# Dense-matmul tiles on 128-byte starts, second MoE in chunks of 384 and 512 tokens, nine x pairs, new planner keys

## The chip, the core and the metric

The kernel runs on one core of a Trainium2 chip. The metric is the device time of one execution in microseconds; lower is better. TensorE (PE) multiplies, VectorE (DVE), ScalarE (ACT) and GpSimd (POOL) do the elementwise work, and SyncE (SP) issues nearly all transfers.

## The reference, cut to what matters

Attention over 4 batches of 8 heads, with a band of 32 positions to each side and 32 global tokens, gives `x` with 4 x 544 = 2176 tokens of 512 features. Two dense blocks follow:

```python
h = np.maximum(x @ w_in, 0.0)                   # 512 -> 1024
conv = sum(conv_w[k] * shifted(h, k - 1) for k in range(3))
x = h * sigmoid(conv) @ w_out                   # 1024 -> 512
xk, xr = (mu * x + (1 - mu) * x_prev for mu in (mu_k, mu_r))
k = np.maximum(xk @ w_k, 0.0)                   # 512 -> 1024
out = sigmoid(xr @ w_r) * (k * k @ w_v)         # 512 -> 512, 1024 -> 512
```

## The kernel before, in words

**Dense matmuls.** Every operand of a dense product is split into a rounded high part and a low rest (`hi`, `lo`, type float32r, 4 bytes an element), and each product is the sum of three matmuls: hi x hi, hi x lo, lo x hi. One matmul holds a 128x128 block as the stationary operand and streams a moving operand of up to 512 columns past it. The five kinds are named by their PSUM tile:

- `ph` (line 955): w_in stationary, the x tiles moving, 482 columns (262 in the last chunk); 480 matmuls
- `po` (line 1044): w_out stationary, the gate tiles `gh`/`gl` moving, 480 columns (260 in the last chunk); 480
- `pk` (line 1187): w_k stationary, `xkh`/`xkl` moving, as many columns as the chunk has tokens; 96 a chunk, 576 in all
- `pr` (line 1251): `xrbuf` stationary, w_r moving, 512 columns; 12 for each of 17 blocks of 128 tokens, 204 in all
- `pv` (line 1288): `k2h`/`k2l` stationary, w_v moving, 512 columns; 24 a block, and 48 of 256 columns for the last block, 432 in all

That is 2172 matmuls with 941,760 columns.

**First MoE.** `dense(b)` works through five chunks of tokens (`CW`, 480 and last 260 wide): `ph` for eight groups of 128 hidden features, then ReLU, a convolution of three taps, sigmoid, product and split on DVE, ACT and POOL, then `po` for four groups, stored to DRAM. The attention of batch b+1 runs in between. An attention unit is two heads: scores `s`, softmax, transposes `pe`, products `o`, normalization `xn`, a transpose `X` (line 633), and copies of `X` into the x pairs of up to two chunks. `XB` = 10 x pairs (ring `x0` for hi, `x1` for lo) are held by four feature blocks of a chunk each until the chunk's last `ph`.

**Second MoE.** `moe2()` cuts the 2176 tokens into chunks of 384, 384, 384, 384, 384 and 256. Each loads its x, forms a difference `d`, the mixes `xk` and `xr` and their splits, then runs all its `pk`, `pr` and `pv` in that order. Behind each of the eight `pk` groups of a chunk stand a ReLU into `robuf` (line 1203), a square (1208), and the split into `k2h` (1215) and `k2l` (1220). The x tiles of this part use the rings `x0` and `x1` too.

**Order of the work.** A planner (`Plan`) simulates the five engines from a cost for each task and emits every engine's order at build time. Among tasks that could start within `WINDOW` it takes the one with the smallest key. Keys are due times: `s_key` for attention (`T_START`, `STEP0`, `T_DENSE`, `SLOT`, `LEAD`, `GAP`, `GAP1`), `d_key` for the dense part, and what these imply for all that they need, transfers included. Elementwise tasks may have two or three engines to go to; the one that finishes first after adding a bias (`DVE_BIAS`, `ACT_BIAS`, `POOL_BIAS`) gets it, with another bias in each phase of time (`PHASES`). `mmr(n)` = n / 2.4 + 13.3 ns is the planner's cost of a dense matmul; a `pr` group of six costs 40 ns more. The order is static: an engine waits at the head of its list.

**Where tiles lie.** Tiles are laid one behind another in SBUF with each size rounded up to 32 bytes. In a partition, the constants end at byte 3360, which is 32 past a multiple of 128, and what follows inherits it. The starts of the dense matmuls' operands, as remainders after division by 128:

| operand | remainder |
|---|---|
| w_in, w_out, later w_v, xrbuf (blocks 512 or 2048 bytes apart) | 32 |
| w_k, w_r | 96 |
| x pairs, 1952 bytes apart: the ring of hi; of lo | 32, 64, 96, 0, 32, ...; 96, 0, 32, 64, ... |
| `gh`/`k2h` (first half; second half, 1928 bytes on) | 32; 40 |
| `gl`/`k2l` (the four buffers; their second halves) | 32, 64, 96, 0; 40, 72, 104, 8 |

For chunk 0 the x tiles of feature blocks k = 0 to 3 start at 32, 64, 32, 0 (hi) and 96, 0, 96, 64 (lo).

Of the kernel before, what the change touches and what calls it, by code (L numbers as in the profile page):

```python
# [10 lines left out]
F32 = mybir.dt.float32  # L11
F32R = mybir.dt.float32r
I32 = mybir.dt.int32
# [6 lines left out]
DM = H * D  # L20
FF = 1024
P = 128
# [5 lines left out]
CW = (480, 480, 480, 480, 260)  # L28
NC = len(CW)
CA = tuple(sum(CW[:c]) for c in range(NC + 1))  # L30
XW = max(CW) + 2
CH0 = 512
XO = max(CW[0] + 1, max(CW[1:]))
TOK = B * S
CH = 384
SCALE = 0.125
BIG = 8.0e9
HUGE = 3.0e38
# [1 line left out]
EST = 256  # L40
# [9 lines left out]
W2_BUFS = 3  # L50
W2R_BUFS = 3
E_STEP = 16
XB = 10
T_START = -32416
STEP0 = 7098
T_DENSE = 24497
SLOT = 58775
LEAD = -7520
GAP = 16998
GAP1 = -7474  # L60
STEPS_H = 6
E_BUFS = 4
H_FRAC = 0.5
LAG_TE = -5130
LAG_PV = 87927
LAG_G = -19574
LEAD_Q = 2184
S_COST = 960
M_COST = 845
E_COST = 1182  # L70
PV_COST = 470
LAG_TX = 11192
WINDOW = 114
FILL_MIN = 309
FILL_MARGIN = 3249
FILL_START = 6
FILL_RATE = 0.624
PENALTY = 4050
AHEAD = 1405
PHASES = (-313483, 41538, 302764, 460459)  # L80
DVE_BIAS = (425, 13181, -112, 8785, 3254)
ACT_BIAS = (-8199, -1203, -224, -20768, -16631)
POOL_BIAS = (24870, -34502, -354, -10831, 5828)
H_BUFS = 5
C_BUFS = 3
G_BUFS = 4
# [330 lines left out]
def mmr(n):  # L417
    return max(119.0, n / 2.4 + 13.3)
# [3 lines left out]
def attn_moe_kernel(  # L422
# [51 lines left out]

    ident = const.tile([P, P], F32, name="ident")
    fold = const.tile([P, 64], F32, name="fold")
    zero = const.tile([P, 1], F32, name="zero")
    mask = const.tile([P, 4, P], F32, name="mask")
    convw = const.tile([P, 3 * FT], F32, name="convw")
    mus = const.tile([P, 2 * KT], F32, name="mus")  # L480
# [174 lines left out]
    def x_alloc(u):  # L655
        b, k = divmod(u, NP)
        for c, *_ in windows(b, 0, S):
            if ("x", c, k) in bufs:
                continue
            bufs["x", c, k] = [buf("x0"), buf("x1")]  # L660
            blank = [z - CA[c] + 1 for z in [GAPPED] + [(S + 1) * i - 1 for i in range(B + 1)] if CA[c] - 1 <= z <= CA[c + 1]]

            def fn(c=c, k=k, blank=blank):
                for i, x in enumerate(bufs["x", c, k]):
                    t = alloc(x, [P, XW], F32R, f"x{i}_{c}_{k}")
                    for z in blank:
                        nc.gpsimd.tensor_copy(t[:, z : z + 1], zero)

            ev["xa", c, k] = add("POOL", 130 * len(blank), fn, take=bufs["x", c, k], name=f"xa{c}_{k}")
            ev["x", c, k] = []  # L670
# [148 lines left out]
    def narrow_tasks(nm, src, n, braw, bmag, after):  # L819
        state = {}  # L820

        def fload():
            state["raw"] = alloc(braw, [P, max(n, EST), 2], I32, f"{nm}r")
            halves = state["raw"].bitcast(I16).rearrange("p n t -> p (n t)")
            part, words = skewed(src), 4 * n - 1
            step = 4 * EST
            for c in range(0, words, step):
                end = min(c + step, words)
                load_to(out=halves[:, c:end], in_=part[:, c:end])

        def fzero():
            state["mag"] = alloc(bmag, [P, max(n, EST)], F32, f"{nm}m")[:, :n]
            nc.gpsimd.memset(state["mag"], 0.0)

        def fhead():
            head = state["mag"].bitcast(F16).rearrange("p (n t) -> p n t", t=2)[:, :, 1]
            top = state["raw"].bitcast(BF16).rearrange("p n (t u) -> p n t u", u=2)[:, :n, 1, 0]
            nc.scalar.copy(head, top)

        def ftail():  # L840
            bits = state["mag"].bitcast(I32)
            nc.vector.scalar_tensor_tensor(
                bits, state["raw"][:, :n, 0], 13, bits, op0=ALU.logical_shift_right, op1=ALU.bitwise_or
            )

        f = n / WST
        a = add("DMA", 1250 * f, fload, deps=after, take=[braw], name=f"ld{nm}")
        z = add("POOL", 150 + 326 * f, fzero, deps=[a], take=[bmag], name=f"zero{nm}")
        c = add("ACT", 60 + 581 * f, fhead, deps=[a, z], use=[bmag, braw], name=f"abs{nm}")
        c = add("DVE", 68 + 534 * f, ftail, deps=[c], use=[bmag, braw], name=f"low{nm}")  # L850
        return c, state
# [221 lines left out]


    outf = out.rearrange("b s d -> (b s) d")
    widths = (384, 384, 384, 384, 384, 256)
    chunks = [(sum(widths[:i]), n) for i, n in enumerate(widths)]
    big = {}

# [14 lines left out]
    def moe2():  # L1094
# [5 lines left out]
        def chunk(ci, tok, n):  # L1100
# [12 lines left out]
            for m in range(KT):  # L1113
                bx, bd = buf("h"), buf("c")

                def fld(bx=bx, m=m):
                    t = alloc(bx, [P, XW + 2], F32, f"x2_{ci}_{m}")
                    for c, lo, hi in spans:
                        lead = int(c == 0)
                        load_to(out=t[:, lo - first : hi - first], in_=x2d[c][m][:, lead + lo - CA[c] : lead + hi - CA[c]])  # L1120

                def fd(e, bx=bx, bd=bd, m=m):
                    d = alloc(bd, [P, XW], F32, f"d{ci}_{m}")
                    e.tensor_sub(d[:, 0 : wd - 1], bx.tile[:, 1:wd], bx.tile[:, 0 : wd - 1])

                src = [ev["x2", c, m] for c, *_ in spans]
                ld = add("DMA", 900, fld, deps=src + [ev["relu", NC - 1]], take=[bx], name=f"ldx{ci}_{m}")
                d = add("DVE", tt(n), lambda fd=fd: fd(nc.vector), deps=[ld], take=[bd], use=[bx], name=f"d{ci}_{m}",
                        alts=[("POOL", 100 + 2.27 * n, lambda fd=fd: fd(nc.gpsimd))])
                for i, nm in ((0, "xk"), (1, "xr")):  # L1130
                    bt = buf("x0")

                    def fx(bt=bt, bx=bx, bd=bd, i=i, nm=nm, m=m):
                        x = alloc(bt, [P, XW], F32, f"xt{ci}{nm}{m}")
                        for o0, i0, sn in segs:
                            nc.vector.scalar_tensor_tensor(
                                x[:, o0 : o0 + sn], bd.tile[:, i0 : i0 + sn], mus[:, KT * i + m : KT * i + m + 1],
                                bx.tile[:, i0 : i0 + sn], op0=ALU.mult, op1=ALU.add,
                            )

                    x = add("DVE", tt(n) + 70, fx, deps=[d], take=[bt], use=[bx, bd], name=f"x{nm}{ci}_{m}")
                    if nm == "xk":
                        bh, bl = buf("x0"), buf("x1")

                        def fh(copy, bh=bh, bt=bt, m=m):
                            copy(alloc(bh, [P, XW], F32R, f"xkh{ci}_{m}")[:, :n], bt.tile[:, :n])

                        def fl(e, bh=bh, bl=bl, bt=bt, m=m):
                            lo = alloc(bl, [P, XW], F32R, f"xkl{ci}_{m}")
                            e.tensor_sub(lo[:, :n], bt.tile[:, :n], bh.tile[:, :n].bitcast(F32))  # L1150

                        h = add("ACT", 40 + act(n), lambda fh=fh: fh(nc.scalar.copy), deps=[x], take=[bh], use=[bt],
                                name=f"xkh{ci}_{m}",
                                alts=[("DVE", 67 + 0.52 * n, lambda fh=fh: fh(nc.vector.tensor_copy))])
                        l = add("DVE", tt(n), lambda fl=fl: fl(nc.vector), deps=[h], take=[bl], use=[bt, bh],
                                name=f"xkl{ci}_{m}", alts=[("POOL", 100 + 2.27 * n, lambda fl=fl: fl(nc.gpsimd))])
                        xk.append([h, l])
                        xkb.append((bh, bl))
                    else:
                        def fh(copy, bt=bt, m=m):  # L1160
                            copy(big["rx"][:, m, :n], bt.tile[:, :n])

                        def fl(e, bt=bt, m=m):
                            e.tensor_sub(
                                big["rx"][:, KT + m, :n], bt.tile[:, :n], big["rx"][:, m, :n].bitcast(F32)
                            )

                        h = add("ACT", 40 + act(n), lambda fh=fh: fh(nc.scalar.copy), deps=[x, free_out] + prev_xr,
                                use=[bt], name=f"xrh{ci}_{m}",
                                alts=[("DVE", 67 + 0.52 * n, lambda fh=fh: fh(nc.vector.tensor_copy))])  # L1170
                        l = add("DVE", tt(n), lambda fl=fl: fl(nc.vector), deps=[h], use=[bt],
                                name=f"xrl{ci}_{m}", alts=[("POOL", 100 + 2.27 * n, lambda fl=fl: fl(nc.gpsimd))])
                        xr.append([h, l])
# [67 lines left out]
            for j in range(nt):  # L1241
# [11 lines left out]
                                start=(k == 0 and i == 0), stop=(k == KT - 1 and i == 2),  # L1253
                            )

                cost = 6 * mmr(DM) + 40
                last = mm_group(
                    f"R{ci}_{j}", bp, 2, part,
                    [[z for k in (2 * q, 2 * q + 1) for z in xr[k] + wrr_done[k, 0]] for q in range(2)],
# [179 lines left out]
```

## Time and profile before

| | |
|---|---|
| runs | 547.84, 551.41, 551.53 us; median 551.41 |
| the profiled execution | 550.57 us, of which its span is 548.8 |
| TensorE busy | 525.0 us, 96% of the span |
| VectorE, ScalarE, GpSimd busy | 321.5, 295.0, 177.4 us |
| mean granted TensorE clock | 0.988 of full speed |

The span runs from the first to the last instruction. Busy time of TensorE counts a matmul until its modelled end, and the ends of neighbours overlap, so the time that a matmul really takes up is the distance from its start to the next one's, called its pace below. The granted clock is 1.00 at 2.4 GHz.

### The profile page before, as it was taken

How to read it: one execution, taken by the hardware profiler on the slowest of the kernel's cores; microseconds unless marked ns; L12 is line 12 of the kernel's file. 1: busy time of each engine (PE TensorE's matmuls, PEld its weight loads, DVE VectorE, ACT ScalarE, POOL GpSimd, SP SyncE). 2: the span in 40 equal slices, each digit the busy share in tenths (PEclk: the TensorE clock that was granted, in tenths of full speed). 3: DMA queues.
4: the chain of work that ended last, by engine and by line, in shares of the span. 5: the costliest groups of instructions: out<-in, count | busy, mean ns of one | idle time of the engine just before them, and what ended most of it. 6: DMA issues, size and time to landing. Idle time of an engine off the chain costs nothing.

```text
span 548.8 us, 12707 instructions
## 1 busy us (share of the span) xinstructions
PE 525.0 (96%) x4952; PEld 453.8 (83%) x4952; DVE 321.5 (59%) x893; ACT 295.0 (54%) x659; POOL 177.4 (32%) x312
## 2 busy tenths in 40 slices
PE   6679997999899999999999999999999999999997
PEld 4568886878678888888899998898898898898896
DVE  3477999378995699629849915628423123161141
ACT  5587978646894689629536665343253143142140
POOL 6145132211212012001000197888887276000000
PEclk9799999999999999999999999999999999999999
DMA  8987857594447700121243624301310100100101
GB/s 308 354 301 238 278 180 240 180 284 152 147 138 225 250 7 13 58 94 39 74 152 81 186 73 134 101 2 44 102 24 31 48 11 18 41 2 0 59 0 39
DMA packets 42237, 64.54 MB, mean 118 GB/s; under 512 B 5569, under 2 KB 34497, under 8 KB 42177
## 3 DMA queue, kind: packets, MB, share of 16 engines
q1 hardware_dynamic: 39296, 59.26, 33.3%
q10 hardware_dynamic: 2880, 4.47, 2.2%
q8 instruction: 39, 0.64, 0.5%
q14 instruction: 22, 0.17, 0.1%
HBM read 51.64 MB, written 12.07 MB: 116 GB/s over the span
## 4 chain that ended last, share of the span: by engine, by line
PE 76%; DVE 7%; POOL 4%; DMA 4%; ACT 4%; issue 3%; SPq 1%; ACTq 0%; DVEq 0%; POOLq 0%
PE ph L955 15%; PE pv L1288 14%; PE po L1044 14%; PE pk L1187 14%; PE pr L1251 7%; DMA kT<-in_k_l_dram 3%; PE o L602 2%; PE s L561 2%; PE pe L592 2%; DVE c L989 2%; POOL wvv_lo L894 1%; PE Xg L757 1%; PE X L633 1%; PE peg L740 1%; POOL k2l L1220 1%
## 5 line engine op out<-in xcount | busy, mean ns | idle before, releaser
L955 PE MATMUL ph<-x,win_hi 128*128 128x482 f32 (+1 forms) x320 | 90.9, 369 | 0.0
L1187 PE MATMUL pk<-xkl,wkk_hi 128*128 128x384 f32 (+1 forms) x192 | 63.2, 329 | 0.2 <-POOL xkl L1150 0.2
L1187 PE MATMUL pk<-xkh,wkk_lo 128*128 128x384 f32 (+1 forms) x192 | 62.9, 328 | 0.0
L1187 PE MATMUL pk<-xkh,wkk_hi 128*128 128x384 f32 (+1 forms) x192 | 62.9, 327 | 0.0
L955 PEld LDWEIGHTS ph<-x,win_hi 128*128 128x128 f32 x320 | 56.5, 189 | 7.2 <-issue 0.6
L1044 PE MATMUL po<-gh,wout_hi 128*128 128x480 f32 (+1 forms) x160 | 60.6, 379 | 1.5 <-DVE e L576 1.5
L1044 PE MATMUL po<-gl,wout_hi 128*128 128x480 f32 (+1 forms) x160 | 58.5, 366 | 0.0
L1044 PE MATMUL po<-gh,wout_lo 128*128 128x480 f32 (+1 forms) x160 | 58.3, 365 | 0.0
L955 PE MATMUL ph<-x,win_lo 128*128 128x482 f32 (+1 forms) x160 | 57.9, 362 | 0.0
L989 DVE SCALAR_TENSOR_TENSOR c<-h,convw,c 128x480 f32<-128x480 f32 (+1 forms) x80 | 52.9, 681 | 6.7 <-ACT c L982 6.4
L1288 PE MATMUL pv<-wvv_lo,k2h 128*128 128x512 f32 (+1 forms) x144 | 55.1, 383 | 0.0
L1288 PE MATMUL pv<-wvv_hi,k2l 128*128 128x512 f32 (+1 forms) x144 | 55.0, 382 | 0.0
L1288 PE MATMUL pv<-wvv_hi,k2h 128*128 128x512 f32 (+1 forms) x144 | 54.8, 381 | 0.0
L1203 ACT ACTIVATE robuf<-pk 128x384 f32<-128x384 f32 (+1 forms) x47 | 22.1, 472 | 60.2 <-PE pk L1187 51.4
L583 ACT ACTIVATE e<-e 128x128 f32<-128x128 f32 x128 | 40.0, 395 | 8.2 <-DVE e L576 8.0
L1251 PE MATMUL pr<-wrr_hi,xrbuf 128*128 128x512 f32 x136 | 43.6, 394 | 0.0
L1301 DVE TENSOR_TENSOR robuf<-pv,robuf 128x512 f32<-128x512 f32 (+1 forms) x18 | 11.9, 659 | 45.2 <-PE pv L1288 45.0
L1187 PEld LDWEIGHTS pk<-xkl,wkk_hi 128*128 128x128 f32 x192 | 36.1, 188 | 1.0 <-POOL xkl L1150 0.6
L576 DVE CUSTOM_DVE_ANT_0 e<-s,mask 128x128 f32<-128x128 f32 x128 | 28.9, 285 | 13.0 <-PE s L561 11.4
L1187 PEld LDWEIGHTS pk<-xkh,wkk_hi 128*128 128x128 f32 x192 | 36.1, 188 | 0.2
L1187 PEld LDWEIGHTS pk<-xkh,wkk_lo 128*128 128x128 f32 x192 | 36.0, 188 | 0.0
L1215 ACT CAST k2h<-robuf 128x384 fp32r<-128x384 f32 (+1 forms) x48 | 23.6, 494 | 21.9 <-POOL robuf L1208 13.2
(194 smaller groups left out, 1131.6 us busy)
## 6 DMA issues: line engine op xcount, KB each, us to landing
v<-in_v_l_dram SPq DMA_DIRECT2D x16, 910.0 KB, 6.6
kT<-in_k_l_dram SPq DMA_DIRECT2D x16, 336.0 KB, 5.3
qT<-in_q_l_dram SPq DMA_DIRECT2D x16, 288.0 KB, 4.7
out_dram<-robuf SPq DMA_DIRECT2D x16, 256.0 KB, 2.0
x2d<-xo ACTq DMA_DIRECT2D x12, 240.0 KB, 3.2
wout_0r<-in_moe_w_out_dram SPq DMA_DIRECT2D x8, 256.0 KB, 3.6
wkk<-wkkd SPq DMA_DIRECT2D x8, 256.0 KB, 3.0
wout_0r<-in_moe_w_out_dram SPq DMA_DIRECT2D x8, 255.8 KB, 4.0
```

Source lines behind the costliest of these rows:

```text
L561: nc.tensor.matmul(s[a][32 * j : 32 * j + 32, i], lhsT=qT[rows[a], q : q + 32], rhs=kT[rows[a], c : c + P], start=(i == 0), stop=True, ski ...
L576: nc.vector.tensor_tensor_reduce(out=e[:, P * i : P * (i + 1)], in0=bs[a].tile[:, i], in1=mask[:, i], scale=-SCALE, scalar=HUGE, op0=ALU.a ...
L583: nc.scalar.activation(be.tile[:, P * i : P * (i + 1)], be.tile[:, P * i : P * (i + 1)], AF.Exp, bias=be.tile[:, SL + i : SL + i + 1], sca ...
L955: nc.tensor.matmul(bp.tile[:, : w + 2], lhsT=wt[:, k, P * m : P * (m + 1)], rhs=x[:, : w + 2], start=(k == 0 and n == 0), stop=(k == KT - ...
L989: e.scalar_tensor_tensor(bc.tile[:, :w], bh.tile[:, k : k + w], convw[:, FT * k + m : FT * k + m + 1], bc.tile[:, :w], op0=ALU.mult, op1=A ...
L1044: nc.tensor.matmul(bp.tile[:, :w], lhsT=wt[:, k, P * m : P * (m + 1)], rhs=g[:, k % 2, :w], start=(k == 0 and n == 0), stop=(k == FT - 1 a ...
L1187: nc.tensor.matmul(bp.tile[:, :n], lhsT=w[:, k, P * m : P * (m + 1)], rhs=x[:, :n], start=(k == 0 and i == 0), stop=(k == KT - 1 and i == 2),)
L1203: e.activation(ks()[:, :n], bp.tile[:, :n], AF.Relu)
L1215: copy(bg[0].tile[:, m % 2, :n], ks()[:, :n])
L1251: nc.tensor.matmul(bp.tile, lhsT=x[:, P * j : P * (j + 1)], rhs=w[:, k], start=(k == 0 and i == 0), stop=(k == KT - 1 and i == 2),)
L1288: nc.tensor.matmul(bp.tile, lhsT=x, rhs=w[:, k, c0:c1], start=(k == 0 and i == 0), stop=(k == FT - 1 and i == 2),)
L1301: nc.vector.tensor_mul(o()[:, c0:c1], bp.tile, r()[:, c0:c1])
```

## The change

1. **Sizes.** `XW`, the width of the x, gate and convolution tiles, goes from 482 to 512 elements (the tile `d` stays wider, at `XW + 2`); `zero` grows from 1 to 32 elements; the raw tiles of the ring `w2raw` get 32 bytes more. The constants then end at 3456 = 27 x 128, the x pairs are 2048 bytes apart, the halves of a gate tile too, and w_k starts at 167,808 = 1311 x 128: every operand of the five kinds starts on a multiple of 128.
2. **Chunks.** The second MoE has chunks of 384, 384, 384, 512 and 512 tokens; `CH`, the width of its PSUM and `robuf` pieces, is 512.
3. **Pairs.** `XB` goes from 10 to 9.
4. **Planner.** New keys, biases and phases, and `pr` groups without the extra 40 ns.

```diff
-XW = max(CW) + 2
+XW = 512
-CH = 384
+CH = 512
-XB = 10
-T_START = -32416
-STEP0 = 7098
-T_DENSE = 24497
-SLOT = 58775
-LEAD = -7520
-GAP = 16998
-GAP1 = -7474
+XB = 9
+T_START = -203492
+STEP0 = 6028
+T_DENSE = 111803
+SLOT = 63566
+LEAD = -4780
+GAP = 13961
+GAP1 = -10557
-H_FRAC = 0.5
-LAG_TE = -5130
-LAG_PV = 87927
-LAG_G = -19574
+H_FRAC = 0.4639
+LAG_TE = -1957
+LAG_PV = 193128
+LAG_G = -16476
-LAG_TX = 11192
-WINDOW = 114
-FILL_MIN = 309
-FILL_MARGIN = 3249
+LAG_TX = 15459
+WINDOW = 125
+FILL_MIN = 1042
+FILL_MARGIN = 2905
-FILL_RATE = 0.624
-PENALTY = 4050
-AHEAD = 1405
-PHASES = (-313483, 41538, 302764, 460459)
-DVE_BIAS = (425, 13181, -112, 8785, 3254)
-ACT_BIAS = (-8199, -1203, -224, -20768, -16631)
-POOL_BIAS = (24870, -34502, -354, -10831, 5828)
+FILL_RATE = 0.605
+PENALTY = 7770
+AHEAD = 1406
+PHASES = (-46811, 40888, 310741, 850557)
+DVE_BIAS = (-32025, 43380, -172, -18857, -14843)
+ACT_BIAS = (-19074, -8449, -234, -21355, 9704)
+POOL_BIAS = (19513, -38192, -377, -35443, 32378)
...
-    zero = const.tile([P, 1], F32, name="zero")
+    zero = const.tile([P, 32], F32, name="zero")
...
-            state["raw"] = alloc(braw, [P, max(n, EST), 2], I32, f"{nm}r")
+            state["raw"] = alloc(braw, [P, max(n, EST) + (4 if braw.ring == "w2raw" else 0), 2], I32, f"{nm}r")[:, : max(n, EST)]
...
-    widths = (384, 384, 384, 384, 384, 256)
+    widths = (384, 384, 384, 512, 512)
...
-                    d = alloc(bd, [P, XW], F32, f"d{ci}_{m}")
+                    d = alloc(bd, [P, XW + 2], F32, f"d{ci}_{m}")
...
-                cost = 6 * mmr(DM) + 40
+                cost = 6 * mmr(DM)
```

## Rows read from the trace of the kernel before

**Rows 1.** The page: busy time, share of the span, instructions.
```profile
PE 525.0 (96%) x4952; PEld 453.8 (83%) x4952; DVE 321.5 (59%) x893; ACT 295.0 (54%) x659; POOL 177.4 (32%) x312
```
**Rows 2.** Busy us of each engine by stage: length, engines, PEclk, DMA share, GB/s.
```profile
0.00:44.10 44.10, 31.89 (x787) 25.71 (x788) 22.64 (x136) 27.39 (x77) 16.14 (x63) 0.88 0.91 318
44.10:111.10 67.00, 62.80 (x774) 52.34 (x773) 55.45 (x159) 52.85 (x118) 20.28 (x45) 0.97 0.66 220
111.10:178.20 67.10, 63.48 (x915) 52.42 (x914) 53.98 (x185) 45.79 (x99) 11.89 (x37) 1.00 0.60 189
178.20:240.90 62.70, 62.53 (x882) 51.91 (x881) 46.44 (x163) 44.42 (x100) 6.83 (x20) 1.00 0.23 76
283.30:295.05 11.75, 11.75 (x97) 11.72 (x97) 7.94 (x20) 8.65 (x22) 0.25 (x1) 1.00 0.10 29
295.05:306.70 11.65, 11.65 (x98) 11.65 (x97) 11.40 (x27) 5.80 (x15) 0.98 (x4) 1.00 0.61 178
332.10:348.80 16.70, 16.70 (x74) 13.50 (x73) 10.73 (x18) 7.99 (x19) 12.81 (x20) 1.00 0.29 90
```
**Rows 3.** The chain that ended last: start, us, instructions.
```profile
242.84 19.70 PE ph L955 x90
262.54 20.96 PE po L1044 x96
...
374.74 16.72 PE pv L1288 x72
...
408.33 8.39 PE pr L1251 x36
...
433.45 16.80 PE pk L1187 x96
...
517.28 11.35 PE pk L1187 x96
```
**Rows 4.** Timeline of TensorE, `ph` of chunk 0, k = 0 to 3: start, us.
```profile
69.59 0.61 PE L955 MATMUL ph<-x,win_hi 128*128 128x482 f32 x2
...
70.26 0.60 PE L955 MATMUL ph<-x,win_hi 128*128 128x482 f32 x2
...
70.91 0.60 PE L955 MATMUL ph<-x,win_hi 128*128 128x482 f32 x2
...
71.57 0.60 PE L955 MATMUL ph<-x,win_hi 128*128 128x482 f32 x2
...
72.23 0.60 PE L592 MATMUL pe<-ident,e 128*128 128x128 f32 x4
```
**Rows 5.** Timeline of TensorE, transposes of plain float32.
```profile
32.19 0.60 PE L633 MATMUL X<-ident,xn 128*128 128x128 f32 x4
32.63 0.60 PE L592 MATMUL pe<-ident,e 128*128 128x128 f32 x4
```
**Rows 6.** Groups of POOL's instructions by shape: busy us, mean ns, idle before.
```profile
L1220 POOL TENSOR_TENSOR k2l<-robuf,k2h 128x384 fp32r<-128x384 f32 x30 | 28.4, 958 | 7.1 <-ACT k2h L1215 7.1
L1208 POOL TENSOR_TENSOR robuf<-robuf 128x384 f32<-128x384 f32 x29 | 24.4, 846 | 12.6 <-ACT robuf L1203 12.6
```
**Rows 7.** Timeline of TensorE: `X` of units 4 and 5, last `ph` of chunk 0.
```profile
67.39 0.60 PE L633 MATMUL X<-ident,xn 128*128 128x128 f32 x4
...
75.08 0.38 PE L955 MATMUL ph<-x,win_lo 128*128 128x482 f32 x1
...
88.46 0.60 PE L633 MATMUL X<-ident,xn 128*128 128x128 f32 x4
```
**Rows 8.** Waits: who waited for what, us in total, times, longest.
```profile
PE s L561 <- DMA kT<-in_k_l_dram: 6.4, 2, 4.1
PE peg L445 <- ACT eT L595: 3.8, 1, 3.8
...
PE pk L1187 <- POOL xkl L1150: 0.2, 1, 0.2
```

More of the change, by code (lines that the diff above doesn't have):

```diff
@@ L666, in fn @@
                     for z in blank:
-                        nc.gpsimd.tensor_copy(t[:, z : z + 1], zero)
+                        nc.gpsimd.tensor_copy(t[:, z : z + 1], zero[:, :1])
             ev["xa", c, k] = add("POOL", 130 * len(blank), fn, take=bufs["x", c, k], name=f"xa{c}_{k}")
```

## The prediction
> **What bounds the kernel now.** I read the page first: TensorE is busy 96% of the span [rows 1]. The stages say where the rest is [rows 2]. Before 44.1 us TensorE works 31.9 us, and its clock is down to 0.88; from there to 240.9 us, where attention and the first MoE interleave, it stands idle for 4.2, 3.6 and 0.2 us; later it never waits. The chain of waits then gives the pace, since from 242.8 us on it is TensorE alone that carries it but for the change from the first to the second MoE, where TensorE is full too [rows 2, 3]. Its longest wait there is 0.2 us for a tile of the second MoE [rows 8]. So time is lost or won where matmuls follow each other closer or wider, and in front of 240.9 us by 20.2 us of idle time at most.
>
> The paces [rows 3]: `ph` 19.70 / 90 = 218.9 ns for 482 columns, `po` 20.96 / 96 = 218.3 for 480, `pk` 16.80 / 96 = 175.0 for 384 and 11.35 / 96 = 118.2 for 256, `pr` 8.39 / 36 = 233.1 and `pv` 16.72 / 72 = 232.2 for 512. The last chunk of the first MoE takes 11.75 and 11.65 us for 96 matmuls each [rows 2], 121.9 ns at 262 and 260 columns. At the granted 2.4 GHz and one column a cycle, the columns would take 200.8, 200, 160, 106.7, 213.3 and 108.8 ns. The excess is 18, 18, 15, 11.5, 19 to 20 and 13 ns: a constant and a part that grows with the columns. Over all of it: 384 x 218.9 + 384 x 218.3 + 192 x 121.9 + 480 x 175.0 + 96 x 118.2 + 204 x 233.1 + 384 x 232.2 + 48 x 118.2 = 429.0 us, where 941,760 columns are 392.4. The excess is 36.6 us in 2172 matmuls.
>
> The sum is made against the profiled execution, 550.57 us (span 548.8 and 1.8 around it); the median of the runs is 0.84 higher, and the forecast is put on the median.
>
> **Sizes.** No pair of operands of the kernel before starts on multiples of 64 on both sides: all stationary blocks of `ph`, `po`, `pk` and the moving operands of `pr`, `pv` lie at 32 or 96. What a moving operand does alone can be read: chunk 0's four feature blocks stream from 32, 96, 32, from 64, 0, 64, from 32, 96, 32 and from 0, 64, 0, and their three matmuls take 0.67, 0.65, 0.66 and 0.66 us [rows 4]. A multiple of 128 on one side alone is worth nothing within the 10 ns of the reading. Both sides at once the trace doesn't show, so the price is bounded. One end is nothing. The other is the whole excess but for what a transpose of plain float32 has: its 128 columns run at two cycles a column (106.7 ns) and four follow in 0.44 us [rows 5], 110 ns, an excess of 3.3 whatever lies where. At one column a cycle the engine must be fed at twice that rate, and only there does an excess that grows with the columns appear; feeding is what starts can change. I take the middle case: the growing part goes and the constant stays, as in the narrow matmuls, 11.5 and 13.1 ns, mean 12.3. Then a matmul takes 213.1 (482), 212.3 (480), 172.3 (384), 225.6 ns (512).
>
> - `ph`: 384 x 5.8 = 2.2 us; `po`: 384 x 6.0 = 2.3; the last chunk 192 x 0.9 = 0.2.
> - `pk`, with the chunks: before 480 x 175.0 + 96 x 118.2 = 95.3; after 288 x 172.3 + 192 x 225.6 = 92.9; gain 2.4.
> - `pr`: 204 x 7.5 = 1.5; `pv`: 384 x 6.6 = 2.5.
>
> That is 11.1 us. The second MoE's 6.4 lies on the path, with the fourth and fifth chunk's 0.2 + a quarter of 4.5 = 1.3. Of the other 3.4, in a stretch where TensorE is busy 188.8 of 196.8 us but the order waits for others too, I count 0.7, 2.4. At the change of MoE DVE works 11.40 of 11.65 us and POOL 12.81 of 16.70 [rows 2], so a `pk` and `pr` that end 0.5 us sooner wait there for it: -0.5. Sum: 6.4 + 1.3 + 2.4 - 0.5 = 9.6 us. The wider stored tiles cost nothing: an instruction of DVE, ACT or POOL still touches only the columns in use.
>
> The Trainium skill speaks to both ends. Its page "SBUF — State Buffer" (Specifications (TRN2)) gives lines of 16 bytes, and a start at 32 or 96 is on such a line already, so by it the sizes change nothing: the first rival's rule; rows 4 agree as far as they reach. Its page "TensorE: Matmul & The Clock Gate" (Back-to-back issue gap) has N / 2.4 + 2.5 ns for a warm matmul, 215.8 at 512 columns, where the trace has 232 and 233; by it the dense matmuls would take 397.6 us after, 31.4 less: the second rival's rule.
>
> **Chunks alone.** One chunk less is 96 `pk` less for the same columns. At the paces of before, with a 512 taken like `pv`: 288 x 175.0 + 192 x 232.2 = 95.0 against 95.3. It is in the sum above; alone it would be 0.3 us. POOL must keep up behind a `pk` group of 512: the square 846 and `k2l` 958 ns at 384 columns [rows 6] become, by the columns, 1.13 + 1.28 = 2.41 us, where TensorE takes 12 x 225.6 = 2.71. The cover is 0.3 us a group, and the four `pr` groups of 2.7 us that stand between the last `pk` and the first `pv`. The new biases leave DVE 16.6 us behind POOL to the end, where the old ones turned to DVE at 460 us, so POOL does this in both wide chunks. Priced at nothing; if POOL also takes the next chunk's `d`, `xkl`, `xrl` in between, `pv` starts some us late.
>
> **Pairs.** The tenth pair matters only where attention is two units ahead before a chunk's `ph` ends. `X` of unit 4 runs at 67.39, the last `ph` of chunk 0 ends at 75.08, and `X` of unit 5 comes at 88.46 [rows 7]: only one pair beyond eight is used, and nine hold it. In the second MoE a chunk's four `xkh`, four of the next and one mix make nine; the mixes go one by one then, over the 16.8 + 8.4 + 16.7 = 42 us of a chunk [rows 3]. Nothing, with that cover.
>
> **Keys.** They order all engines anew. What is to be had is the 20.2 us of idle time, of which 12.2 are in front of 44.1 us where the DMA engines are 91% busy [rows 2]; what can be lost is one more wait like the longest, 4.1 us for a load and 3.8 for ScalarE [rows 8]. I take 0 and keep 4 us to each side. The lower cost of `pr` moves only the plan.
>
> **The rivals.** (1) Nothing comes of the starts: the excess belongs to float32r at one column a cycle, or to the loading of blocks. For it: rows 4. Then 0.3 us of the chunks and the keys remain: 551, from 547 to 555. (2) The full pace: an excess of 3.3 ns as in rows 5, 2076 x 3.3 + 392,400 ns = 399.3 us, 29.7 less, of which 3.0 of the attention stretch's share is lost: 551.4 - 26.7 = 525. Against it: the narrow matmuls keep 11.5 to 13. (3) Equal starts collide: stationary and moving block now have the same remainder always, which in rows 4 two matmuls of three have at k = 0 and 2 (32 beside w_in's 32) and none at k = 1 and 3. The former take 0.665 and the latter 0.655 us on average, 5 ns for each that shares. All 2076 sharing: 10.4 us, 562. It decides if `pr` and `pv` go above 233. Against it: the difference is as large as the reading's last digit.
>
> **How the numbers follow.** Forecast, 0.56: 551.4 - 9.6 = 541.8, with 4 us for the keys and 3 for the constant, 535 to 548. Nothing from the starts 0.18, full pace 0.13, collision 0.07, and 0.06 for an order that loses more than 5 us by POOL or the front. The range to hold 8 in 10 runs from 527 to 553: the upper half of the full pace and all of the first rival but its tail are inside. About 1% (5.5 us) is what a measurement of this kernel can tell from no change. Faster by more: 0.46 of the forecast, 0.13 of the full pace, 0.04 of the first rival, 0.02 elsewhere, 0.65. Within: 0.09 + 0.12 + 0.01 + 0.01 = 0.23. Slower: 0.12.
>
> **What would show it.** In the chain after: 36 `pr` in 8.1 us, 72 `pv` in 16.2, 96 `pk` of 512 columns in 21.7 and of 384 in 16.5, `ph` at 213 ns. Paces as before speak for the first rival, 216 ns at 512 columns for the second, above 233 for the third. `X` of the second unit of a batch waiting for a last `ph` would show the ninth pair short; `pv` waiting for POOL's `k2l` would show the wide chunks' cover gone; idle time of TensorE before 240 us other than some 20 us is the keys'. The forecast is wrong if paces stay or if that idle time grows by the gain.

## The result, and the profile after

The change made the kernel faster: 535.21 us median (533.85 to 536.92) against 551.40 before, ratio 0.9723 with a 95% interval of 0.9675 to 0.9771. The forecast, 541.8, had the sign and the range (527 to 553), but its 9.6 us were 16.2. The profiled execution of after is 535.16 us with a span of 533.3, 15.5 less than before's.

First the page, then busy time by stage, in the columns of [rows 2]; the cuts are again the first `ph` of each chunk, the first `po` and `pk`.

```profile
PE 517.2 (97%) x4846; PEld 441.7 (83%) x4846; DVE 312.4 (59%) x880; ACT 284.5 (53%) x624; POOL 189.3 (35%) x300
```

```profile
0.00:44.20 44.20, 32.59 (x787) 25.91 (x788) 22.15 (x133) 27.33 (x77) 15.49 (x61) 0.88 0.88 303
44.20:105.10 60.90, 59.93 (x734) 49.48 (x732) 54.18 (x158) 49.84 (x109) 19.69 (x41) 1.00 0.71 229
105.10:170.60 65.50, 65.10 (x955) 53.37 (x954) 55.14 (x190) 44.21 (x105) 14.83 (x40) 1.00 0.65 195
170.60:231.60 61.00, 61.00 (x874) 51.25 (x873) 48.92 (x169) 45.74 (x94) 9.96 (x27) 1.00 0.29 95
...
421.00:475.40 54.40, 54.40 (x242) 45.05 (x241) 6.79 (x7) 14.83 (x26) 27.16 (x22) 1.00 0.05 20
```

Against [rows 2]: the front is as long as it was. The three chunks of the first MoE that run beside attention take 60.9 + 65.5 + 61.0 = 187.4 us where they took 196.8. The fourth and fifth chunk, from 231.6 to 297.1, lose 0.3 us together, and the second MoE, from 297.1 to the end, is 236.2 us where it was 242.1. So 9.4 of the 15.5 us are in the stretch where TensorE used to wait, and 5.9 in the second MoE.

The chain that ended last shows the paces (start, us, instructions; before's are [rows 3]):

```profile
233.51 19.80 PE ph L955 x90
253.31 20.82 PE po L1044 x96
...
314.23 8.20 PE pr L1251 x36
322.43 16.32 PE pv L1288 x72
338.75 16.66 PE pk L1187 x96
...
421.12 21.76 PE pk L1187 x96
442.88 10.88 PE pr L1251 x48
```

`pv` went from 232.2 to 226.7 ns, `pr` from 233.1 to 227.8 (226.7 in the wide chunks), `pk` of 384 columns from 175.0 to 173.5, and a `pk` of 512 takes 226.7. But `po` of 480 columns went only from 218.3 to 216.9, and `ph` of 482 from 218.9 to 220.0. The excess over the columns at 2.4 GHz is 13.3 to 13.5 ns where 384 or 512 columns stream (14.5 for `pr` in the narrow chunks), 17 at 480 and 19 at 482.

The waits of TensorE (who for what, us in total, times, longest; before's are [rows 8]):

```profile
PE s L561 <- DMA kT<-in_k_l_dram: 4.2, 1, 4.2
PE o L602 <- issue: 3.6, 2, 2.8
```

The wait for ScalarE's `eT` is gone as a loss. In the kernel before, the timelines of TensorE and of ScalarE show it (start, us):

```profile
88.90 0.60 PE L592 MATMUL pe<-ident,e 128*128 128x128 f32 x4
93.30 1.38 PE L445 MATMUL peg<-ident 128*128 128x128 f32 x10 [3.81 <-ACT eT L595]
```

```profile
85.16 1.28 ACT L713 ACT_TABLE_LOAD   x1
...
87.39 1.14 ACT L891 CAST wout_hi<-wout_0m 128x512 fp32r<-128x512 f32 x2
...
89.04 1.28 ACT L995 ACT_TABLE_LOAD   x1
...
92.67 0.58 ACT L595 COPY eT<-pe 128x512 f32<-128x512 f32 x1
```

TensorE stood 3.8 us and then ran ten fill matmuls (matmuls that the planner puts in to keep TensorE busy, and whose product nobody reads), because ScalarE had two loads of its tables, two parts of w_out and other work in its list ahead of that copy. That wait cost more than itself. The fills hold the next useful matmul back by 1.2 us, and then the granted clock is at its lower level, 1.2 GHz (length, busy, clock, DMA share, GB/s):

```profile
94.80:98.00 3.20, 3.20 (x10) 0.50 0.35 118
```

Eight `po` of 480 columns take 3.35 us there, from 94.79 to 98.14, where eight at 218 ns take 1.74: another 1.6 us. With the 3.8 it makes 6.6 us that hang on one wait. From 44 us to the end of the matmuls after's granted clock is 1.00 throughout. After, ScalarE has both copies done before it turns to the table:

```profile
83.42 1.06 ACT L595 COPY eT<-pe 128x512 f32<-128x512 f32 x2
...
90.95 1.28 ACT L713 ACT_TABLE_LOAD   x1 [0.38 <-DVE eg L708]
```

### The profile page after: what moved, and what is told of

Its sections match the earlier page's. It is cut to its first block, busy times and chain, and to the rows that moved or that the text cites. A ratio compares the mean times of both kernels' runs of the same rounds, so it can differ in the third digit from the quotient of the medians.

```text
span 533.3 us, 12435 instructions
## 1 busy us (share of the span) xinstructions
PE 517.2 (97%) x4846; PEld 441.7 (83%) x4846; DVE 312.4 (59%) x880; ACT 284.5 (53%) x624; POOL 189.3 (35%) x300
## 4 chain that ended last, share of the span: by engine, by line
PE 91%; DMA 3%; DVE 2%; issue 1%; ACT 1%; SPq 1%; ACTq 0%
PE ph L955 18%; PE pk L1187 18%; PE pv L1288 17%; PE po L1044 16%; PE pr L1251 9%; PE s L561 3%; PE o L602 3%; PE pe L592 2%; DMA kT<-in_k_l_dram 2%; PE sg L696 1%; PE Xg L757 1%; PE X L633 1%; PE peg L740 1%; DMA x2d<-xo 1%; SPq L441 1%
## 5 line engine op out<-in xcount | busy, mean ns | idle before, releaser
L1187 PE MATMUL pk<-xkl,wkk_hi 128*128 128x384 f32 (+1 forms) x160 | 57.1, 357 | 0.0
L1187 PE MATMUL pk<-xkh,wkk_lo 128*128 128x384 f32 (+1 forms) x160 | 57.0, 356 | 0.0
L1187 PE MATMUL pk<-xkh,wkk_hi 128*128 128x384 f32 (+1 forms) x160 | 57.0, 356 | 0.0
L1203 ACT ACTIVATE robuf<-pk 128x384 f32<-128x384 f32 (+1 forms) x39 | 20.7, 532 | 54.7 <-PE pk L1187 51.6
L1208 POOL TENSOR_TENSOR robuf<-robuf 128x384 f32<-128x384 f32 (+1 forms) x32 | 30.6, 960 | 34.0 <-ACT robuf L1203 34.0
L1220 POOL TENSOR_TENSOR k2l<-robuf,k2h 128x384 fp32r<-128x384 f32 (+1 forms) x32 | 38.1, 1198 | 12.7 <-ACT k2h L1215 12.4
L1215 ACT CAST k2h<-robuf 128x384 fp32r<-128x384 f32 (+1 forms) x39 | 21.7, 556 | 28.8 <-POOL robuf L1208 26.1
L955 PEld LDWEIGHTS ph<-x,win_lo 128*128 128x128 f32 x160 | 30.2, 189 | 4.0
```

What stands on the lines that cost most here:

```text
L955: nc.tensor.matmul(bp.tile[:, : w + 2], lhsT=wt[:, k, P * m : P * (m + 1)], rhs=x[:, : w + 2], start=(k == 0 and n == 0), stop=(k == KT - ...
L1187: nc.tensor.matmul(bp.tile[:, :n], lhsT=w[:, k, P * m : P * (m + 1)], rhs=x[:, :n], start=(k == 0 and i == 0), stop=(k == KT - 1 and i == 2),)
L1203: e.activation(ks()[:, :n], bp.tile[:, :n], AF.Relu)
L1208: e.tensor_mul(ks()[:, :n], ks()[:, :n], ks()[:, :n])
L1215: copy(bg[0].tile[:, m % 2, :n], ks()[:, :n])
L1220: e.tensor_sub(bg[1].tile[:, m % 2, :n], ks()[:, :n], bg[0].tile[:, m % 2, :n].bitcast(F32))
```

## The experiments

Two theories stood against each other. The first: operands on common starts shorten only matmuls of 384 and 512 columns, which is, with the wide chunks, the 5.9 us of the second MoE, and the 9.4 us of the stretch are the new order's. The rival: the starts made all of it. Each time below stands beside the kernel before on the same chip, 550.4 us for the first four, 551.0 for the next four, 550.7 for the last three.

**Starts alone, and pairs alone.** `e1_sizes` is before with part 1 of the change and nine pairs; `e4_xb9` is before with nine pairs. The planner uses no width of a tile, so both run the same order.

```diff
# both
-XB = 10
+XB = 9
# e1_sizes only
-XW = max(CW) + 2
+XW = 512
...
```

> The kernel before with the sizes alone: operands on multiples of 128, and nine pairs, without which they don't fit; old chunks, old keys. Theory (the starts shorten only matmuls whose columns fill whole lines: 384, 512 and 256; 480 and 482 hardly): in the profile pr and pv at 227 ns, pk at 173.5, po at 217, ph at 220; the second MoE about 5.5 us shorter, before it less than 1 us; about 545 us. Rival (the 7 us that the attention stretch lost between the two kernels are of the starts too, because other engines read and write faster): about 537.

> The kernel before with nine pairs, nothing else. Its order of instructions is that of e1_sizes, so the two differ by the starts alone. Theory: paces as before (pr and pv 232 to 233), 549 to 553 us. Rival (the pairs were what the stretch between 44 and 241 us waited for): that stretch shortens by 5 us or more, 544 to 546.

`e1_sizes`: 543.23 us, ratio 0.988 (0.9855 to 0.9905). `e4_xb9`: 546.47, ratio 0.9925 (0.9898 to 0.9951). Chain of `e1_sizes`, then of `e4_xb9`:

```profile
238.62 21.13 PE ph L955 x96
...
320.24 8.20 PE pr L1251 x36
328.44 16.32 PE pv L1288 x72
```

```profile
239.38 21.14 PE ph L955 x96
...
321.66 8.39 PE pr L1251 x36
330.05 16.70 PE pv L1288 x72
```

At one order, the starts take `pr` and `pv` from 233 and 232 to 228 and 227 ns, and leave `ph` at 220.1 and 220.2. What they don't touch is the stretch; busy time of TensorE from the first `ph` to that of the fourth chunk in `e1_sizes`, then `e4_xb9`, then before and after (length, busy, clock, DMA share, GB/s):

```profile
42.30:238.40 196.10, 189.72 (x2574) 0.99 0.52 168
```

```profile
43.40:239.10 195.70, 189.72 (x2572) 0.99 0.52 168
```

```profile
44.10:240.90 196.80, 188.81 (x2567) 0.99 0.50 164
```

```profile
44.20:231.60 187.40, 186.03 (x2558) 1.00 0.55 174
```

So the first theory holds. The second MoE of `e1_sizes` takes 237.8 us (241.3 in `e4_xb9`, 242.1 before): 3.5 us for the starts at one order, and 4.3 against before, where 5.5 were expected. `pk` of 256 columns, which the theory had among the shortened, went up instead, from 11.31 to 11.51 us for 96. The time of `e1_sizes` came 2 us below what was expected because `e4_xb9` missed: 4 us less than before where I had 549 to 553. The rival of `e4_xb9` has no support either, since the stretch is 1.1 us shorter, not 5. Its profile has another 0.7 us less in front, 0.3 in the last chunks and 0.8 in the second MoE, and its runs spread over 4.1 us. Nine pairs give another order; more the runs don't settle.

**The starts taken back.** `e2_scatter` is after with tiles 520 columns wide (2080 bytes apart) and the constants and raw tiles of before, so chunks, keys and order are after's.

```diff
-XW = 512
+XW = 520
-    zero = const.tile([P, 32], F32, name="zero")
+    zero = const.tile([P, 1], F32, name="zero")
...
```

> The kernel after with its starts scattered again: tiles 520 columns wide, so 2080 bytes apart, constants and raw tiles as before; operands start at 32, 64, 96 or 0 past multiples of 128, stationary blocks at 32 and 96. Chunks, keys and order are those of after. Theory: pr and pv back at 232 to 233, pk of 512 near 232, of 384 at 175; the second MoE 5 to 6 us longer, the stretch before it as after within 1.5 us; 540.5 to 542.5. Rival (all of the gain is the starts'): 549 to 552.

539.79 us, ratio 0.9809 (0.9786 to 0.9832): 4.6 us over after. Its stretch and its chain:

```profile
43.30:231.40 188.10, 185.93 (x2557) 1.00 0.54 171
```

```profile
233.69 19.65 PE ph L955 x90
...
356.50 8.40 PE pr L1251 x36
...
423.73 22.08 PE pk L1187 x96
...
456.99 22.31 PE pv L1288 x96
```

`pr` and `pv` are back at 233 and 232, `pk` of 512 at 230.0. The stretch stays short, 188.1. And `ph` is 218.3 ns with scattered starts, no more than after's 220.0: at 482 columns common starts bring nothing. Both halves of the first theory are shown by this one run, though its size was put too high: the second MoE is 240.9 us, 4.7 longer than after's where 5 to 6 were expected, and the time is 0.7 below the range given.

**Which starts.** Three runs keep after's order and move one side of SBUF: `e5_left32` puts all but w_k and w_r at 32 (`zero` one element wide), `e6_left64` at 64 (16 elements), and `e7_right96` leaves all at 0 but puts w_k and w_r at 96.

```diff
# e5_left32; e6_left64 has 16
-    zero = const.tile([P, 32], F32, name="zero")
+    zero = const.tile([P, 1], F32, name="zero")
# e7_right96
-max(n, EST) + (4 if braw.ring == "w2raw" else 0), 2]
+max(n, EST), 2]
```

> The kernel after with the constants 96 bytes shorter: everything of the left side (x, gates, w_in, w_out, w_v, xrbuf) starts at 32, all at equal remainders; w_k and w_r stay at 0. Order and plan are after's. Theory (both operands must start on a multiple of 128, or of 64): all five kinds at the paces of before, pv and pr near 232 to 233, pk of 512 at 230 to 232; about 540. Rival (only the remainders of the two must be equal): pv at 227 as after, pr and pk of 512, whose operands now differ by 32, at 231 to 233.

> As e5_left32 with the left side at 64. Theory (a multiple of 64 is enough): all paces as after, pv and pr at 227, pk of 512 at 227; 535. Rival (it must be 128): paces as before, 540.

> The kernel after without the 32 bytes in the raw tiles: only w_k and w_r start at 96, all else at 0. In pk the stationary operand is off, in pr the moving one. Theory (one operand off is enough to lose it all): pk of 512 at 230 to 232 and pr at 233, pv at 227; about 537. Rival 1 (the moving operand alone decides): pk at 227, pr at 233. Rival 2 (the stationary one alone decides): pk at 231, pr at 227.

538.66, 536.44 and 538.90 us, one execution each. Chains of the fourth chunk of the second MoE, in that order:

```profile
422.45 22.49 PE pk L1187 x96
444.94 11.21 PE pr L1251 x48
456.14 21.80 PE pv L1288 x96
```

```profile
420.71 22.40 PE pk L1187 x96
443.11 11.00 PE pr L1251 x48
454.12 21.77 PE pv L1288 x96
```

```profile
422.57 22.49 PE pk L1187 x96
445.06 11.21 PE pr L1251 x48
...
```

With both operands at 32, `pv` keeps 227.1 ns, and at 64 it has 226.8: it is not the multiple of 128. `pk` and `pr`, whose operands are now 32 apart, take 234 ns and 233.5, whichever of the two was moved. So my theory in `e5_left32` fell and its rival holds: stationary and moving operand must start at the same remainder. In `e6_left64`, 64 apart, `pk` pays all (233.3) and `pr` a third (229.2), so neither of its two expectations fits; why the two differ is open. In `e7_right96` the theory holds: one operand off is enough (`pk` of 512 is at 234.3, above the 232 that was expected). It says little about the side, though. Moving less stationary start, after 128 bytes, is 32 in `pk` and 96 in `pr` both here and in `e5_left32`, and the paces are the same. Narrower `pk` feels it less: in `e7_right96` the second and third chunk's 96 of 384 columns take 16.65 us each, as after, and only the first chunk's are slower (17.04 us for 95, after 16.76).

That a pair of operands starts alike is not enough by itself. In the kernel before, the first halves of `k2h` start at 32 as w_v does (see the table of starts), while other blocks of the same stream do not. From one start to the next in the trace, the 144 `pv` of 512 columns with such a pair take 232.3 ns on average, and the other 235 take 232.4. In `e2_scatter` it is 96 `pv` at 231.7, against 232.7 for the rest. These runs show the gain only where all matmuls of a kind have it; what makes a mixed stream lose it is open. Nor is 128 shown to be the divisor: 3456 and 167,808 leave the same remainder after 512 too, so after has equal starts by either, and `pr` before, 64 apart by 128 as in `e6_left64`, takes 233.1 ns where that run has 229.2.

**Chunks.** `e3_oldwidths` is after with `widths = (384, 384, 384, 384, 384, 256)`.

> The kernel after with the old chunks of the second MoE (384 five times, 256). Theory: 96 pk more for the same columns at 13.3 ns of constant each, 1.3 us; 535.5 to 538. Rival (the wide chunks relieve POOL, DVE and ACT): 3 us or more, 538 to 541.

535.89 us, ratio 0.9734 (0.9712 to 0.9757), 0.7 over after's median, which the runs can't tell apart. In the chain the last chunk is

```profile
502.39 11.51 PE pk L1187 x96
```

at 119.9 ns, 13.2 of it excess. So the wide chunks save a constant of 13 ns for each of 96 matmuls, and no more; the rival has nothing.

**Full columns in the first MoE.** `e8_wide510` is after with other chunks in the first MoE, an attempt at a version faster than both.

```diff
-CW = (480, 480, 480, 480, 260)
+CW = (510, 510, 510, 510, 140)
```

> The kernel after with chunks of 510, 510, 510, 510 and 140 tokens in the first MoE, so that ph has 512 columns (and 142), po 510 (and 140). Theory (an aligned matmul of 512 columns costs 13.3 ns beside its columns, one of 482 costs 19): ph at 227 and, in the last chunk, at 72 to 74: 4 x 227 + 73 = 981 against 4 x 220 + 120 = 1000 ns, 96 times, 1.8 us less; po of 510 between 227 and 231, so within 1 us of after; in all 533 to 536 if the plan, whose keys were not set for it, loses nothing. Rival (the widths upset the plan): 538 or more, with idle time of TensorE before the last chunk.

545.61 us, ratio 0.9897 (0.9855 to 0.994): the rival. Its stretch up to the second chunk's first `ph`, then of its chain the fourth chunk's `ph`:

```profile
42.50:110.20 67.70, 65.58 (x803) 0.97 0.70 232
```

```profile
243.16 20.45 PE ph L955 x90
```

That `ph` is at 227.2 ns for its 512 columns, as expected, and `po` of 510 at 226.7. But the first stretch is 67.7 us long where after's is 60.9 and the three together 198.7: the wider chunks need more work there (TensorE is busy for 65.58 us, after 59.93), and keys set for other widths plan it worse.

The last chunk's `ph` missed what was expected of it, 72 to 74 ns:

```profile
285.37 6.00 PE ph L955 x54
```

That is 111 ns for 142 columns, which take 59.2 at 2.4 GHz. So a matmul here has a least time that its columns don't set, and the narrow ones of 256 to 262 columns, at 118 to 122 ns, are not far above it. (The planner's cost has such a least too: in the code `mmr(n)` is the larger of 119 and n / 2.4 + 13.3 ns.)

**Which keys.** Three runs put one group of after's keys back to its old values.

```diff
# e9_olddue: T_START, STEP0, T_DENSE, SLOT, LEAD, GAP, GAP1, H_FRAC and the LAG_ keys, as
-T_DENSE = 111803
+T_DENSE = 24497
...
# e10_oldbias: PHASES, DVE_BIAS, ACT_BIAS, POOL_BIAS, as
-PHASES = (-46811, 40888, 310741, 850557)
+PHASES = (-313483, 41538, 302764, 460459)
...
# e11_oldrest: WINDOW, FILL_MIN, FILL_MARGIN, FILL_RATE, PENALTY, AHEAD, as
-PENALTY = 7770
+PENALTY = 4050
...
```

> The kernel after with the old due times (T_START to GAP1, H_FRAC and the LAG_ keys), everything else new; operands stay on 128. Theory (the due times are what took TensorE's waits of 4 and 3 us out of the stretch from 44 to 241 us): that stretch, from the first ph to the first ph of the fourth chunk, is 195 us or more, where after has 187.4; the second MoE as after, 233; 542 or more. Rival (the biases or the thresholds did it): within 2 us of after, 534 to 537.5.

> The kernel after with the old biases and phases of the choice of engine. Theory (due times alone matter; before 303 us the biases rank the engines as before): stretch within 2 us of after's 187.4, second MoE within 1 us of 233; 534 to 538. Rival (the shares of DVE, ACT and POOL made the room): stretch 192 or more, 540 or more.

> The kernel after with the old WINDOW, FILL_ thresholds, PENALTY and AHEAD, among them the cost of changing ScalarE's table. Theory (due times alone matter): within 2 us of after, 534 to 538. Rival (fewer fills and table changes made the room: the kernel before has 10 fills at 93 us): fills return in the stretch, 1 us for ten, and it is 190 or more; 538 or more.

`e9_olddue`: 543.15 us, ratio 0.9859 (0.9826 to 0.9893). `e10_oldbias`: 536.25, 0.9728 (0.9693 to 0.9762). `e11_oldrest`: 542.94, 0.9855 (0.9821 to 0.9888). Stages from the first `ph` of one chunk to that of the next, chunks 0 to 2 (`e9_olddue`, then `e11_oldrest`):

```profile
44.30:107.00 62.70, 58.07 (x572) 0.97 0.69 227
107.00:179.90 72.90, 70.54 (x1176) 1.00 0.59 193
179.90:241.20 61.30, 61.30 (x818) 1.00 0.21 71
```

```profile
43.30:104.50 61.20, 56.48 (x570) 1.00 0.70 228
104.50:177.50 73.00, 70.72 (x1113) 1.00 0.61 192
177.50:240.10 62.60, 62.24 (x880) 1.00 0.23 78
```

Either group put back loses the whole 9.4 us: the stretch is 196.9 and 196.8 long. Fewer of attention's matmuls then run beside the first chunk (572 and 570 against 734 in after), TensorE waits 4.6 and 4.7 us there, and they follow in the next stage. (The kernel before has 774 there, ten of them fills, so their number alone doesn't decide.) So the theory that due times alone did it fell with `e11_oldrest`, and the fills and table changes did not do it either: no fill returned, and ScalarE loads its tables 20 times in the whole run against 22 after. What in the plan makes the room, with both groups new, stays open. The biases are worth little: `e10_oldbias` is within 2 us of after, though its stretch is 191.4, 4.0 us longer than after's and more than the theory allowed; a front of 42.5 us makes up 1.7 of it.

## Why the prediction was right, and where it was not

- **What bounds the kernel**: held. TensorE's paces and its 8.0 us of waits between 44 and 241 us were the two places, and both gave. A third was left out: the granted clock behind a wait, 1.6 us from 94.8 us on, which rows 2 show as 0.97 in that stage.
- **Common starts, 512 and 384 columns**: that a growing part of the excess goes with the starts was right, the size nearly. I took a constant of 12.3 ns from the narrow matmuls; 13.3 to 13.5 was measured. That is partly luck: the middle case was a choice between two bounds, and `e8_wide510` shows that narrow matmuls stand near a least time, so their excess is no measure of a constant. For the same reason rows 5 don't bound it: 110 ns for 128 columns need not be two cycles a column. The second MoE was to lose 6.4 - 0.5 us, and lost 5.9. This agreement is partly luck too: by the paces `pk` gives 1.8, `pr` 1.2 and `pv` 2.1, 5.1 us in all where 6.4 were put down, the chunks' 1.3 among them; the other 0.8 came from outside the paces.
- **Common starts, 480 and 482 columns**: this term failed. 4.5 us were put down for `ph` and `po`; by the paces it is 384 x (218.9 - 220.0) + 384 x (218.3 - 216.9) = 0.1 us. The constant of narrow matmuls was carried over to every width. That cost the sum 2.4 + 1.1 us. What stands at these widths is an excess of 17 to 19 ns that the starts don't touch.
- **Rows 4 as evidence**: a wrong reading. It showed that `ph` doesn't mind where its moving operand starts, and I made of it that one side alone is worth nothing for all kinds. `ph` minds nothing at all (at one order 220.2 scattered and 220.1 common). The sentence is true for `pk` of 512 and `pr`, but `e7_right96` shows that, not rows 4.
- **Sizes named by their multiple of 128**: I argued with the change's own number. `e5_left32` shows that equal remainders are what counts, as far as all matmuls of a kind have them. The third rival, that equal starts collide, is thereby the reverse of what happens at 512 columns; at 482, from which it was read, nothing of its 5 ns shows at one order.
- **Keys at 0, 4 us to each side**: mis-sized; they gave 9.4. I took the longest single wait, 4.1 or 3.8 us, as the measure, and idle time as all that was to be had. But 8.0 us of idle time lay outside the front, and the new plan took 6.6 of them away (196.8 - 188.81 before, 187.4 - 186.03 after) and 2.8 us of busy time besides, which the prediction put at nothing: 1.2 us of fills and 1.6 us at the lower clock, both behind the wait for `eT`. That wait was worth 6.6 us, not 3.8.
- **Nine pairs**: no wait of TensorE came of them. They show elsewhere: POOL, which blanks a new pair, waited for a chunk's last `ph` as it releases one (2.4 us before),

```profile
POOL x L667 <- PE ph L955: 7.2, 4, 6.1
```

  7.2 us of POOL's time that nobody waited for. That a smaller ring would give another plan, worth some us either way (`e4_xb9`), was not in the step.
- **Wide chunks and POOL**: held. I had worked out 1.28 and 1.13 us for `k2l` and the square of 512 columns:

```profile
L1220 POOL TENSOR_TENSOR k2l<-robuf,k2h 128x512 fp32r<-128x512 f32 x16 | 21.5, 1346 | 8.0 <-ACT k2h L1215 8.0
...
L1208 POOL TENSOR_TENSOR robuf<-robuf 128x512 f32<-128x512 f32 x16 | 16.6, 1040 | 27.3 <-ACT robuf L1203 27.3
```

  1.35 + 1.04 = 2.39 us for a `pk` group of 2.72, and TensorE is busy 54.4 of the 54.4 us of the fourth chunk.
- **The change of MoE**: 0.5 us were held back for a wait that hardly grew. The first chunk's 96 `pk` take 16.99 us after, 0.3 over their pace, and took 17.04 before, 0.2 over.
- **The Trainium skill's two rules**: by the lines of 16 bytes (page "SBUF — State Buffer", Specifications (TRN2)) the starts would change nothing; at 512 columns 5 to 8 ns a matmul speak against it as a rule for float32r. By N / 2.4 + 2.5 ns (page "TensorE: Matmul & The Clock Gate", Back-to-back issue gap) 512 columns would take 215.8; the best here is 226.7.

The errors offset in part. From the 9.6 us, 3.5 come off for the first MoE's matmuls and 0.5 for the second's, and 9.4 for the plan and 0.5 for the wait come on: 15.5, the difference of the two spans.

## What to carry to other kernels

Where float32r matmuls of 512 columns follow each other, compare the starts of the two operands: some 6 ns each are to be had by bringing all of a stream's operands to the same remainder, which here needed wider tiles and a few unused bytes ahead of them. Read such an effect from the kind that you want to shorten, not from a neighbour of another width. And where engines run a planned static order, treat its keys as one set: a term of its own, since any change of a ring or a cost makes another plan and moves some us by itself. Its bound is the idle time and what hangs on it, the fills and the matmuls at the lower clock behind a wait.

## What the runs showed of the hardware that was not expected

- All of a kind's operands at equal remainders after 128 bytes: 226.7 ns for 512 columns, at 0, and 226.8 to 227.1 at 64 and 32; 32 apart, 234 for `pk` and 233.5 for `pr`; 64 apart, 233.3 and 229.2. Equal pairs among unequal ones, in `pv` before: 232.3.
- The effect depends on the number of columns: 5 to 8 ns at 512, 1.5 at 384 between before and after, none at 482. At 256 the sign turns: `pk` takes 119.9 ns with common starts (`e3_oldwidths`) and 118.2 before.
- At common starts, 384 columns (173.5) and 512 (226.7) keep 13.3 to 13.5 ns over the columns at 2.4 GHz; 480 keep 17 and 482 keep 19, and 510 take as long as 512 (226.7). Why is open: the runs varied starts, and of widths only 510 and 512.
- A narrow matmul has a least time: 142 columns took 111 ns, 52 more than the columns. What sets it is open.
- After TensorE stood idle for 3.8 us and ran 1.2 us of fills, its granted clock was 0.50 from 94.8 to 98.0 us, and `po` took some 400 ns instead of 218.
